# Sigmoid attention and a gated feed-forward on one core: four f chunks of the first batch done as seven block products, and a bank order in the late pairs

## The chip, the cores and the metric

One core of a Trainium2 chip runs the whole program; the other cores do nothing. The metric is the device time of one execution in microseconds (us). A core has a matrix engine (TensorE, PE in the profile; its weight loads are a row of their own, PEld), a vector engine (VectorE, DVE), a scalar engine (ScalarE, ACT), GpSimd (POOL), which here only issues DMAs and a tiny copy, and SyncE (SP), which issues the stores and the DMA transposes. Each engine works through its own instructions in the order in which the program gives them; semaphores tie the engines together. Matrix products land in PSUM, which this kernel uses as eight banks of 128 rows by 512 fp32 columns.

## The reference

```python
def _attn_ref(q, k, v):                      # 8 batches, 12 heads, 448 tokens, 64 deep
    S = q.shape[2]
    scale = 1.0 / np.sqrt(q.shape[-1])
    scores = scale * np.matmul(q, k.transpose(0, 1, 3, 2)) - np.log(S)
    attn = 1.0 / (1.0 + np.exp(-scores))
    return np.matmul(attn, v).astype(np.float32)

def _moe_ref(x, w_gate, w_val, w_out):       # 3584 tokens, 768 wide, 1536 inner
    gate = np.maximum(x @ w_gate, 0.0)
    val = x @ w_val
    return (gate * val @ w_out).astype(np.float32)

def reference(**kwargs):
    ...
    attn_out = _attn_ref(**attn_kwargs)
    B, H, S, D = attn_out.shape
    x = np.ascontiguousarray(attn_out.transpose(0, 2, 1, 3)).reshape(B * S, H * D)
    return _moe_ref(x=x, **moe_kwargs)
```

There is no softmax: each score goes through a sigmoid by itself. All inputs and the output are fp32; the kernel multiplies in fp16 and accumulates in fp32.

## The kernel before

**Attention.** A batch is 3 groups (g) of 4 heads by 7 chunks (c) of 64 keys for each half of the heads: 21 score units. `qk_unit` (L299) makes one: 4 matmuls of 64 by 64 by 448 columns (`qk`, L233) into two banks, and two sigmoids on ScalarE (L187) that write the tile PT. After a group's seven units `pv` (L249) multiplies PT with the values, 28 matmuls in 64-row pieces into two banks, and `put_xT` (L172) copies them to xT on VectorE (L184). Queries and keys are needed transposed: for batches 0 and 1 TensorE does that (`transposed`, L198; `both` is two calls of it), for later batches VectorE gathers them into a tile `rel` (L222, two buffers) and SyncE issues a DMA transpose of it (L226, `dma_transposes`).

**Feed-forward up.** The inner dimension is 12 chunks f of 128. For a chunk and a run of tokens the plain form is `gv` (L311): six matmuls for the gate product g_ps and six for the value product v_ps, one bank each (L322), a relu of g_ps into `gate_sb` on ScalarE (L334) or, when `act_relu` is false, on VectorE (L336), and one VectorE product of gate_sb and v_ps into hT (L343). Here this last one is called the gating product.

Most of it is done instead by a scheme that replaces eight block products by seven, with sums of blocks made beforehand on VectorE: for pairs of batches (`gv_pair`, L594), for the down projection (`down_pair`, L448), and for one batch alone, whose 448 tokens are cut into two halves of 224 (`gv_split`, L688). `gv_split` treats four f chunks at once. Gate and value weights are two block rows, the two halves of the 768 inputs are the block columns; the tokens' two halves are the columns of the other operand. It needs:

- `split_sums(b)` (L674): four sums of xT's blocks into a tile that takes one of xT's three buffers.
- weight sums, four steps for two chunks (`early_sum_steps`, L556): `gate_sums` replaces wv's upper half by wg − wv **in place**, then S2, S1 and S4. After the first of them a plain `gv` of these chunks is no longer possible. The sums take the SBUF of the first batch's old PT tiles.
- six banks, named u, g2 and g1 (p, c and a in the code), two each: every product is 12 matmuls of 224 columns, two chunks to a bank. The products are numbered by their weight set: 0, 3, 4, 1, 5, 6, 2. The products 0, 4, 5 and 2 add up in u, 3 and 6 in g2, 1 stands in g1. Between them the running values are copied out of the banks (`copy`, L719) or added to fp32 tiles `gsb` (`plus`, L723), and at the end four gating products (L729) write hT.

Before the change `gv_split` serves batch 1 alone: chunks 0 to 3 and 4 to 7, in batch 2's stretch. Batch 0 is done entirely in plain form.

**Banks.** `bank()` (L77) hands out the bank at the front of a ring of eight and moves it to the end; a new user waits for the last reader of the bank it gets. `later(order)` (L85) moves the named banks to the end again, so that they come back later. In the order list 0 to 7 are places in the ring, 7 the one handed out last.

**What stands beside what.** The main loop (L924) runs batch by batch. A batch's 21 score units are cut into bursts; behind each burst comes feed-forward work of earlier batches. For batch 1 (the *stretch* of this text) the cuts are after 3, 6, 9, 13, 17 and 21 units, with a `pv` inside the fourth and the sixth burst. Behind the bursts `ffn_mix` (L764) takes `mix` = 4, 3, 3, 3, 3, 4 plain units of batch 0 from a queue: four units of the second token half (192 tokens; the first half has 256) for f 0 to 3, then f 4 to 11 in pairs of chunks, first half and second half in turn. Two of them, (first half, f 9) and (second half, f 8), have their relu on VectorE. Between units `hooks` place the transposes of batch 1's groups (`both`) and batch 2's DMA transposes; `late_loads` (L863) does batch 2's third DMA transpose, a small copy on POOL that waits for the second (`hold`), and then issues batch 2's values, batch 3's keys and queries and w_out. `steps` and `given` spread the sixteen weight-sum steps, which batch 1's split work needs later, over the mixes in the order of the chunks.

**Loads.** All big loads are DMAs issued from POOL's queue in program order (L113, L115, L117, L149); `load_gv(f0, f1)` brings the gate and value weights of some chunks.

**Late pairs.** In batches 5 and 7 a `down_pair` is interrupted by a burst of three score units (`amid`). For the pairs in `SUMS_LATE` (L403) its tail is: product b with S3, an addition and a scaling of it on VectorE, a new bank d, `later((0, 7))`, the last two sum steps of the next pair, product d and its addition (L489 to L501). The next burst follows: two score units, a `pv`, two score units.

Of the kernel before, what the change touches and what calls it, by code (L numbers as in the profile page):

```python
# [18 lines left out]
def kernel(  # L19
# [10 lines left out]
    nc = tc.nc  # L30
# [46 lines left out]
    def bank(name, shape=(P, 512), dtype=FP32):  # L77
        pool, tag = free[0]
        free.rotate(-1)
        return pool.tile(list(shape), dtype, tag=tag, name=name)  # L80
# [4 lines left out]
    def later(order):  # L85
        keys = [free[i - 8] for i in order]
        for key in keys:
            free.remove(key)
            free.append(key)
# [55 lines left out]
    def load_gv(f0, f1, which=(0, 1)):  # L145
        fs = slice(f0 * P, f1 * P)
        for i in which:
            wt, src = ((wg, moe_w_gate), (wv, moe_w_val))[i]
            nc.gpsimd.dma_start(wt[:, :, fs], src[:, fs].rearrange("(c p) f -> p c f", p=P))  # L149
# [4 lines left out]
    load(1, 0, 1, "kq")  # L154
    load_gv(4, 6)
    load(1, 1, 2, "kq")
    load_gv(6, 9)
    load_v(1)
    load(1, 2, 3, "kq")
    load_gv(9, 12)  # L160

    def load_o():
        for f0, f1 in ((0, HF), (HF, NFC)):
# [186 lines left out]
    def store(g, t, ysb, m0, m1, engines):  # L350
        if len(engines) == 1:
            b, c = 2 * g + 2 * t // NCH, 2 * t % NCH
            dst = out[b * S : (b + 1) * S, m0:m1].rearrange("(t c) m -> c t m", c=NCH)[c : c + 2]
            engines[0].dma_start(dst, ysb[:, m0:m1])
            return
        for i, eng in enumerate(engines):
            j = 2 * t + i
            b, c = 2 * g + j // NCH, j % NCH
            dst = out[b * S : (b + 1) * S, m0:m1].rearrange("(t c) m -> c t m", c=NCH)[c]
            eng.dma_start(dst, ysb[64 * i : 64 * i + 64, m0:m1])  # L360
# [87 lines left out]
    def down_pair(g, p, beside, then, last, first_copy, amid=None):  # L448
# [14 lines left out]
        def plus(o, ps):  # L463
            nc.vector.scalar_tensor_tensor(  # L464
                out=o, in0=ps[:, 0:HM], scalar=OUT_SCALE, in1=o, op0=AOP.mult, op1=AOP.add
            )
# [6 lines left out]
        if (g, p) in SUMS_LATE:  # L473
            product(a, A12, B21)
            plus(y1[:, lo], a)
            product(c, S1, T1)
            scaled_act(y2[:, hi], c)
            product(b, S2, T2, False)
            scaled_act(y1[:, hi], b)
            product(c, S4, B22, False)  # L480
            plus(y1[:, hi], c)
            store(*first, y1, 0, DM, (nc.sync, nc.sync))
            steps = ()
            if amid:
                amid()
                steps = prepare_steps()
                for step in steps[:2]:
                    step()
            product(b, S3, T3, False)  # L489
            plus(y2[:, hi], b)  # L490
            (scaled if amid else scaled_act)(y2[:, lo], b)
            d = bank("y21")
            if amid:
                later((0, 7))
                for step in steps[2:]:
                    step()
            else:
                then()
            product(d, A22, T4)
            plus(y2[:, lo], d)  # L500
            store(*second, y2, 0, DM, (nc.sync, nc.sync))  # L501
            return
        product(c, S1, T1)
# [181 lines left out]
        sub(T4, B21, T2)  # L685
        sub(T3, B22, B12)

    def gv_split(b, f, beside):  # L688
        x = xT_tiles[b]
        T1, T2, T4, T3 = split_X[b]  # L690
        B11, B21, B22 = x[:, 0:HD, 0:SQ], x[:, HD:NDC, 0:SQ], x[:, HD:NDC, SQ:S]
        p, c, a = ([bank(nm) for _ in range(2)] for nm in ("u", "g2", "g1"))
        later((6, 7, 4, 5, 2, 3))
        gs = [[gsbp.tile([P, S], FP32, tag="gsb", name="gsb") for _ in range(3)] for _ in range(2)]
        h = hT_tiles[b // 2]
        sets = []
# [20 lines left out]
        def copy(i, ps, by=nc.scalar.copy):  # L717
            for u in range(2):
                by(gs[u][i][:], ps[u][:, 0:S])  # L719
# [12 lines left out]
            )  # L732

        product(p, 0, B11)
        copy(0, p, nc.vector.tensor_copy)
        product(c, 3, T1)
        copy(2, c)
        product(p, 4, T2, False)
        copy(1, p)
        beside()  # L740
        product(a, 1, B21)
        plus(0, a)
        product(p, 5, T3, False)
        plus(2, p)
        product(c, 6, B22, False)
# [14 lines left out]
    def push_first(half, fs, act_relu=True):  # L760
        c0, c1 = HALVES[half]
        push_gv(0, 64 * c0, 64 * (c1 - c0), fs, act_relu)
# [76 lines left out]
                after[(i, u)]()  # L839
    slots[5].pv()  # L840
    push_first(1, range(0, 4))
    for f0 in range(4, 12, 2):
        for half in range(2):
            for f in range(f0, f0 + 2):
                push_first(half, (f,), (half, f) not in ((0, 9), (1, 8)))


    order = [(g, c) for g in range(NG) for c in range(NCH)]
# [75 lines left out]
    for b in range(1, B):  # L924
# [10 lines left out]
        count = len(bursts)  # L935
        hooks = {}
        if b == 1:
            mix = (4, 3, 3, 3, 3, 4)
            hooks = {
                1: [(3, lambda: both(1, 1))],  # L940
                3: [(3, lambda: both(1, 2))],
                4: [(2, lambda: dma_transposes(2, 0)), (0, lambda: dma_transposes(2, 1))],
                5: [(4, late_loads)],
            }
            steps = itertools.chain.from_iterable(early_sum_steps(j, 2 * j) for j in range(4))
            given = ((0, 0, 1, 1, 1), (0, 1, 1, 1), (0, 1, 1, 1), (0, 1, 1, 0), (2, 0, 0, 0), (0, 1, 1, 1, 0))
        else:
            mix = (0,) * count

# [106 lines left out]
```

## Time and profile before

| | us |
|---|---|
| median of 3 executions | 389.37 (389.04 to 389.99) |
| the profiled execution | 388.7 |
| its span, first to last instruction | 386.9 |
| batch 1's stretch, first score product to batch 2's | 28.9 to 61.2 |

Busy time in parts of the span, from the view of windows (us):

| window | PE | DVE | ACT | POOL |
|---|---|---|---|---|
| 7.0 to 28.9 | 21.40 | 11.39 | 18.07 | 12.41 |
| 28.9 to 61.2 | 32.30 | 21.70 | 24.43 | 8.62 |
| 61.2 to 98.0 | 36.80 | 28.27 | 26.00 | 8.62 |
| 98.0 to 224.0 | 125.99 | 106.87 | 83.08 | 13.95 |

The granted TensorE clock is 1.00 in all of them. A matmul's recorded duration holds its way through the array, and matmuls overlap; what one costs is the distance from its start to the next one's start. The same holds for ScalarE and VectorE: the sigmoids of a burst overlap a little. In a timeline row stand the start, the length of the merged group, engine, line, operation, tiles and shapes, the count, and in brackets idle time before it and what ended it.

### The profile page before, as it was taken

To read this page: it belongs to the slowest core of one execution; us is meant where nothing else is said; L and a number is where in the kernel's file an instruction comes from. 1 tells how busy PE (TensorE), PEld (TensorE's weight loads), DVE (VectorE), ACT (ScalarE), POOL (GpSimd) and SP (SyncE) were. 2 spreads that over 40 slices of the span, in tenths; PEclk is the share of its full clock that TensorE was granted. 3 is DMA by queue.
4 is the path that set the end of the run, shared out by engine and by line. 5 is a ranking of instruction groups with operands and counts; after the bars stand their busy time and mean duration, and the time that the engine had idled before them with its cause. 6 is when DMAs were issued, how large, how long until landed. Compare 5 with 4: busy or idle time off the path is not lost.

```text
span 386.9 us, 8977 instructions
## 1 busy us (share of the span) xinstructions
PE 381.3 (99%) x3570; PEld 224.8 (58%) x3570; DVE 304.3 (79%) x609; ACT 227.5 (59%) x480; POOL 49.9 (13%) x73
## 2 busy tenths in 40 slices
PE   8999999999999999999999999999999999999995
PEld 6688776885555545555555554545555555555563
DVE  3455667769868999999867789999987788999563
ACT  5967887567777645555777764545577344333321
POOL 9543306100400003000300300000000000000000
PEclk9999999999999999999999999999999999999999
DMA  9999999999969303972599893222012220000336
GB/s 177 197 199 204 203 192 162 208 208 128 184 148 193 81 2 38 156 120 47 50 230 223 160 232 56 49 48 50 0 43 71 69 69 0 2 0 0 83 88 160
DMA packets 67421, 43.81 MB, mean 113 GB/s; under 512 B 35634, under 2 KB 64050, under 8 KB 67378
## 3 DMA queue, kind: packets, MB, share of 16 engines
q0 software_dynamic: 28960, 23.24, 39.9%
q1 hardware_dynamic: 37634, 19.24, 24.7%
q10 hardware_dynamic: 784, 0.75, 0.6%
q8 instruction: 28, 0.46, 0.5%
q14 instruction: 15, 0.12, 0.1%
HBM read 47.19 MB, written 11.01 MB: 150 GB/s over the span
## 4 chain that ended last, share of the span: by engine, by line
PE 97%; ACT 2%; DVE 0%; issue 0%
PE u L385 35%; PE g L385 16%; PE y L385 12%; PE qk_ps L239 10%; PE pv_ps L257 8%; PE g_ps L322 5%; PE v_ps L322 5%; PE u L708 2%; PE g L708 2%; ACT PT L187 2%; PE warm_ps L175 1%; PE trt L204 1%; DVE ysb L540 0%; DVE zeros L130 0%
## 5 line engine op out<-in xcount | busy, mean ns | idle before, releaser
L187 ACT ACTIVATE PT<-qk_ps 128x448 f16<-128x448 f32 (+3 forms) x318 | 151.2, 583 | 78.8 <-PE qk_ps L239 78.6
L385 PEld LDWEIGHTS <-S 128*128 128x128 f16 x576 | 56.4, 98 | 45.9
L624 DVE TENSOR_TENSOR gsb<-g,gsb 128x448 f32<-128x448 f32 x72 | 42.8, 624 | 8.0 <-PE g L385 7.7
L239 PE MATMUL qk_ps<-qkT 64*64 64x448 f16 (+2 forms) x756 | 47.8, 336 | 0.5 <-ACT PT L187 0.3
L385 PEld LDWEIGHTS <-hT 128*128 128x128 f16 x318 | 29.5, 98 | 24.0 <-issue 6.1
L257 PE MATMUL pv_ps<-PT,v 64*64 64x448 f16 (+2 forms) x756 | 37.0, 329 | 0.0
L464 DVE SCALAR_TENSOR_TENSOR ysb<-y,ysb 128x384 f32<-128x384 f32 x33 | 18.3, 555 | 20.8 <-PE y L385 14.3
L184 DVE TENSOR_SCALAR xT<-pv_ps 128x448 f16<-128x448 f32 (+2 forms) x53 | 27.8, 567 | 8.2 <-PE pv_ps L257 7.1
L385 PEld LDWEIGHTS <-wg 128*128 128x128 f16 x216 | 20.2, 98 | 21.8 <-issue 4.3
L385 PEld LDWEIGHTS <-wv 128*128 128x128 f16 x216 | 21.1, 98 | 19.7
L446 ACT ACTIVATE ysb<-u 128x384 f32<-128x384 f32 x28 | 13.8, 491 | 30.6 <-PE u L385 26.5
L239 PEld LDWEIGHTS <-qkT 64*64 64x64 f16 x756 | 18.3, 106 | 20.3 <-issue 13.8
L385 PE MATMUL u<-wo,hT 128*128 128x384 f16 x156 | 29.8, 327 | 0.0
L111 POOL DMA_DIRECT2D k<-in_k_dram x14 | 10.8, 775 | 141.6 <-DVE rel L222 136.0
L257 PEld LDWEIGHTS <-v 64*64 64x64 f16 x756 | 22.5, 107 | 10.3 <-issue 1.1
L385 PE MATMUL u<-xT,wg 128*128 128x448 f16 x108 | 23.5, 354 | 0.0
L385 PE MATMUL g<-X,S 128*128 128x448 f16 x108 | 23.4, 352 | 0.0
L385 PE MATMUL u<-xT,wv 128*128 128x448 f16 x108 | 23.4, 352 | 0.0
L385 PE MATMUL u<-X,S 128*128 128x448 f16 x108 | 23.4, 352 | 0.0
L385 PE MATMUL g<-xT,wg 128*128 128x448 f16 x108 | 23.4, 353 | 0.0
L385 PE MATMUL u<-X,wv 128*128 128x448 f16 x108 | 23.4, 352 | 0.0
L385 PE MATMUL g<-xT,S 128*128 128x448 f16 x108 | 23.4, 352 | 0.0
(98 smaller groups left out, 563.5 us busy)
## 6 DMA issues: line engine op xcount, KB each, us to landing
out_dram<-ysb SPq DMA_DIRECT2D x50, 192.0 KB, 3.9
v<-in_v_dram POOLq DMA_DIRECT2D x8, 336.0 KB, 15.7
v<-in_v_dram POOLq DMA_DIRECT2D x16, 168.0 KB, 15.4
k<-in_k_dram POOLq DMA_DIRECT2D x4, 672.0 KB, 12.3
q<-in_q_dram POOLq DMA_DIRECT2D x4, 672.0 KB, 15.6
wo<-in_moe_w_out_dram POOLq DMA_DIRECT2D x2, 1152.0 KB, 19.0
k<-in_k_dram POOLq DMA_DIRECT2D x9, 224.0 KB, 11.9
q<-in_q_dram POOLq DMA_DIRECT2D x7, 224.0 KB, 12.3
```

Source lines behind the costliest of these rows:

```text
L111: nc.gpsimd.dma_start(t16[:, xs, cs], rows_of(src, b)[:, xs, cs])
L175: nc.tensor.matmul(ps[:, 0:n], zeros[:, 0:P], zeros[:, 0:n], start=True, stop=True)
L184: nc.vector.tensor_scalar(out=xT, in0=src, scalar1=XSCALE, scalar2=None, op0=AOP.mult)
L187: nc.scalar.activation(PT_ap, ps_ap, AF.Sigmoid, bias=sig_bias, scale=qk_scale)
L239: nc.tensor.matmul(out_of(hh)[o : o + 64, :], qkT[rows, c, cols], qkT[rows, NCH + c0 : NCH + c1, cols], start=True, stop=True, tile_positi ...
L257: nc.tensor.matmul(ps[hh][64 * r : 64 * r + 64, 0:qn], v16[rows, 2 * g + hh, c * D : (c + 1) * D], pieces[c][rows, hh, :], start=(c == 0), ...
L322: nc.tensor.matmul(ps[:, 0:qn], (wg, wv)[i][:, dc, f * P : (f + 1) * P], xT_tiles[b][:, dc, q0 : q0 + qn], start=(dc == 0), stop=(dc == ND ...
L385: nc.tensor.matmul(ps[:, 0:n], A[:, k_, :], W[:, k_, :], start=(first and k_ == 0), stop=(k_ == kn - 1), skip_group_check=True,)
L446: nc.scalar.activation(o, ps[:, 0:HM], AF.Copy, scale=OUT_SCALE)
L464: nc.vector.scalar_tensor_tensor(out=o, in0=ps[:, 0:HM], scalar=OUT_SCALE, in1=o, op0=AOP.mult, op1=AOP.add)
L624: nc.vector.tensor_tensor(out=gs[u][i][:], in0=ps[u][:, 0:S], in1=gs[u][i][:], op=AOP.add)
L708: nc.tensor.matmul(ps[j // 2][:, j % 2 * SQ : (j % 2 + 1) * SQ], sets[j][i][:, k_, :], W[:, k_, :], start=(first and j % 2 == 0 and k_ == ...
```

## The change

It does in batch 1's stretch four chunks of batch 0, f 4 to 7 with all 448 tokens, by `gv_split` (behind the third burst), in place of eight plain units. The mixes become 2, 1, 1, 2, 3 and 3 units; the queue holds f 0 to 3 of the second half, then f 8 and 9 and f 10 and 11 for both halves, all with the relu on ScalarE. `split_sums(0)` goes ahead of the first unit. The sum steps come in the order of chunks 4, 6, 0, 2, since chunks 4 to 7 are used first and chunks 0 to 3 must stay plain until their units are done; the last four steps for f 6 stand around the start of the split work. For this use `gv_split` gets a variant, `sums_late`: products in the order 0, 1, 3, 4, 5, 6, 2, the copy of product 0 on ScalarE, and the banks asked for and put back in another order. The hooks move: `both(1, 2)` stays behind the fourth burst, the first two DMA transposes of batch 2 stand after two and three of the fifth mix's three units (before: after one and three), `late_loads` stays at the head of the sixth mix. Weights are loaded as chunks 6 to 7, 8 to 9 and 10 to 11 in place of 6 to 8 and 9 to 11.

In the late pairs `later((0, 7))` becomes `later((0, 6, 7))`, and the next pair's last two sum steps come behind the addition of product d instead of ahead of product d.

```diff
-    load_gv(6, 9)
+    load_gv(6, 8)
     load_v(1)
     load(1, 2, 3, "kq")
-    load_gv(9, 12)
+    load_gv(8, 10)
+    load_gv(10, 12)
...
             d = bank("y21")
             if amid:
-                later((0, 7))
-                for step in steps[2:]:
-                    step()
+                later((0, 6, 7))
             else:
                 then()
             product(d, A22, T4)
             plus(y2[:, lo], d)
+            for step in steps[2:]:
+                step()
             store(*second, y2, 0, DM, (nc.sync, nc.sync))
             return
...
-    def gv_split(b, f, beside):
+    def gv_split(b, f, beside, sums_late=False):
...
-        p, c, a = ([bank(nm) for _ in range(2)] for nm in ("u", "g2", "g1"))
-        later((6, 7, 4, 5, 2, 3))
+        if sums_late:
+            p, a, c = ([bank(nm) for _ in range(2)] for nm in ("u", "g1", "g2"))
+            later((4, 5, 6, 7, 2, 3))
+        else:
+            p, c, a = ([bank(nm) for _ in range(2)] for nm in ("u", "g2", "g1"))
+            later((6, 7, 4, 5, 2, 3))
...
         product(p, 0, B11)
-        copy(0, p, nc.vector.tensor_copy)
+        copy(0, p, nc.scalar.copy if sums_late else nc.vector.tensor_copy)
+        if sums_late:
+            product(a, 1, B21)
+            plus(0, a)
+            beside()
         product(c, 3, T1)
         copy(2, c)
         product(p, 4, T2, False)
         copy(1, p)
-        beside()
-        product(a, 1, B21)
-        plus(0, a)
+        if not sums_late:
+            beside()
+            product(a, 1, B21)
+            plus(0, a)
         product(p, 5, T3, False)
...
-    for f0 in range(4, 12, 2):
+    for f0 in (8, 10):
         for half in range(2):
-            for f in range(f0, f0 + 2):
-                push_first(half, (f,), (half, f) not in ((0, 9), (1, 8)))
+            push_first(half, (f0, f0 + 1))
...
         if b == 1:
-            mix = (4, 3, 3, 3, 3, 4)
+            mix = (2, 1, 1, 2, 3, 3)
+            steps = itertools.chain.from_iterable(early_sum_steps(j, 2 * j) for j in (2, 3, 0, 1))
+
+            def some_sums(n):
+                for step in itertools.islice(steps, n):
+                    step()
+
+            def first_split():
+                some_sums(3)
+                gv_split(0, 4, lambda: some_sums(1), True)
+
             hooks = {
-                1: [(3, lambda: both(1, 1))],
-                3: [(3, lambda: both(1, 2))],
-                4: [(2, lambda: dma_transposes(2, 0)), (0, lambda: dma_transposes(2, 1))],
-                5: [(4, late_loads)],
+                0: [(2, lambda: split_sums(0))],
+                1: [(1, lambda: both(1, 1))],
+                2: [(0, first_split)],
+                3: [(2, lambda: both(1, 2))],
+                4: [(1, lambda: dma_transposes(2, 0)), (0, lambda: dma_transposes(2, 1))],
+                5: [(3, late_loads)],
             }
-            steps = itertools.chain.from_iterable(early_sum_steps(j, 2 * j) for j in range(4))
-            given = ((0, 0, 1, 1, 1), (0, 1, 1, 1), (0, 1, 1, 1), (0, 1, 1, 0), (2, 0, 0, 0), (0, 1, 1, 1, 0))
+            given = ((0, 0, 1), (1, 1), (1, 0), (0, 1, 1), (1, 1, 0, 1), (0, 1, 1, 1))
```

## The prediction

> **What bounds the kernel now.** I read the page's busy times and chain of waits first, then the timelines of TensorE (PE), ScalarE (ACT) and VectorE (DVE) through batch 1's stretch, 28.9 to 61.2 us, and TensorE's around the pairs that the second edit touches.
>
> ```profile
> PE 381.3 (99%) x3570; PEld 224.8 (58%) x3570; DVE 304.3 (79%) x609; ACT 227.5 (59%) x480; POOL 49.9 (13%) x73
> ...
> PE 97%; ACT 2%; DVE 0%; issue 0%
> ```
>
> The chain is TensorE almost alone, so a product left out is worth its time and a wait put in front of TensorE costs its time. The change does both. First TensorE: two plain products of 256 and of 192 columns, the existing split work of batch 1, and two weighted-sum rounds (pv) followed by eight score products (qk).
>
> ```profile
> 36.59 0.82 PE L322 MATMUL g_ps<-xT,wg 128*128 128x256 f16 x6
> 37.24 0.82 PE L322 MATMUL v_ps<-xT,wv 128*128 128x256 f16 x6
> 37.90 0.66 PE L322 MATMUL g_ps<-xT,wg 128*128 128x192 f16 x6
> 38.39 0.66 PE L322 MATMUL v_ps<-xT,wv 128*128 128x192 f16 x6
> ...
> 66.48 1.32 PE L708 MATMUL u<-xT,wg 128*128 128x224 f16 x12
> 67.64 1.31 PE L708 MATMUL g<-X,S 128*128 128x224 f16 x12
> 68.79 1.31 PE L708 MATMUL u<-X,S 128*128 128x224 f16 x12
> ...
> 182.91 1.49 PE L257 MATMUL pv_ps<-PT,v 64*64 64x448 f16 x28
> 184.24 0.55 PE L239 MATMUL qk_ps<-qkT 64*64 64x448 f16 x8
> 184.72 1.15 PE L385 MATMUL u<-wo,hT 128*128 128x384 f16 x6
> ...
> 192.85 1.62 PE L257 MATMUL pv_ps<-PT,v 64*64 64x448 f16 x28
> 194.17 0.68 PE L239 MATMUL qk_ps<-qkT 64*64 64x448 f16 x8
> 194.78 1.15 PE L385 MATMUL u<-wo,hT 128*128 128x384 f16 x6
> ```
>
> Start to start counts, since a group's length holds its drain: 0.655 us for a 256-column product, 0.495 for 192, 1.15 for twelve 224-column matmuls. Then the two engines that empty the banks:
>
> ```profile
> 29.39 2.72 ACT L187 ACTIVATE PT<-qk_ps 128x448 f16<-128x448 f32 x6 [0.62 <-PE qk_ps L239]
> 31.96 0.83 ACT L334 ACTIVATE gate_sb<-g_ps 128x192 f32<-128x192 f32 x3
> ...
> 50.32 3.60 ACT L187 ACTIVATE PT<-qk_ps 128x448 f16<-128x448 f32 x8 [0.59 <-PE qk_ps L239]
> ```
>
> ```profile
> 32.38 0.62 DVE L343 TENSOR_TENSOR hT<-gate_sb,v_ps 128x192 f16<-128x192 f32 x2 [2.62 <-ACT gate_sb L334]
> ...
> 51.77 0.42 DVE L336 TENSOR_SCALAR gate_sb<-g_ps 128x256 f32<-128x256 f32 x1 [0.34 <-PE g_ps L322]
> ...
> 52.76 0.39 DVE L222 COPY rel<-k 128x896 f16<-128x896 f16 x1
> ...
> 58.18 0.40 DVE L222 COPY rel<-k 128x896 f16<-128x896 f16 x1 [0.80 <-DMA qkT<-rel]
> ```
>
> Sigmoids follow each other by (31.96 − 29.39)/6 = 0.43 us, and a relu of a unit waits its turn behind all sigmoids of the burst before it. VectorE's gating product waits for that relu (2.62 us here) and everything behind it on VectorE waits too. Today four-unit mixes give TensorE enough to do meanwhile, and in the burst of eight sigmoids VectorE takes the relus itself (51.77).
>
> **Term 1, products removed.** Eight units, 4 × 2 × (0.655 + 0.495) = 9.20 us, become seven products, 7 × 1.15 = 8.05: **−1.15 us**. Bursts, and with them the 0.1 us at each turn between 64- and 128-row work, stay six.
>
> **Term 2, ring order.** From 192.85 to the u product is 1.93 us, from 182.91 it is 1.81: the pv's second bank is that of the burst's sixth sigmoid, which ends at 192.91. The same 0.12 to 0.13 stands at 202.91 and 289.93. The new order gives pv the bank that VectorE's scaling empties at 192.60; the step sums, 0.47 each, then run behind the last addition, before pv's own copies at 194.38. 3 × 0.13 = **−0.39 us**; bounds 0 and −0.4.
>
> **Term 3, waits added.** The trace shows none of the new stretch, so I walk it bank by bank: eight banks handed round, each engine in program order, with spacings 0.43 us a sigmoid, 0.21 and 0.26 a relu, 0.19 a score unit, 0.27 and 0.33 a gating product. The same walk over today's order ends at 61.05 where the trace has 61.11 (the 61.20 start less the 0.1 turn).
>
> (a) *Second burst.* Until 31.6 nothing differs. Two units now stand between the bursts instead of four, so the second burst starts at 31.69. Its second score unit needs the banks of sigmoids five and six, ended 32.12 and known at TensorE 0.05 later (wanted 31.88); its third needs the first unit's, freed by the gating product of 32.38 + 0.35 = 32.73, known at 32.79 (wanted 32.36). 0.29 + 0.43 = **+0.72**, nearly read off the trace.
>
> (b) *S1 of chunks 6 and 7.* ScalarE goes from sigmoids to sigmoids: the third burst's six begin at 35.5, its relu comes at 38.0, the gating product ends at 38.7. Only then may VectorE do the three steps that open the split work (gate sums, S2, S1). Each reads the one before, and then an operation starts 0.03 us after its predecessor's end (X's sums start at 64.21 and 64.74, 0.50 long), so 0.55 + 0.03 each: S1 is there at 40.4. TensorE starts the split at 36.7, and 2 × 1.15 + 0.58 later, 39.5, wants it: **+0.88**.
>
> (c) *Products 4 and 5.* Both add into u and stand next to each other now; batch 1's version has the g1 product between. Half of product 4 is done 0.17 (drain) + 0.07 after its issue, ScalarE's copy takes 0.58 (L719's mean) + 0.06 to tell: 0.88, of which product 4's other half covers 0.58: **+0.30**. Bounds 0 and 1.15.
>
> (d) *Sixth burst.* All relus are ScalarE's now. The fifth burst's eight sigmoids, from 52.2, end their turn at 55.6; VectorE stands before the first gating product until 56.0, then has a sum step, then the second product, done 57.1. The sixth burst's pv wants that bank at 56.6: **+0.54**.
>
> (e) *Into batch 2.* Behind that same product stand the copies for batch 2's first DMA transpose: 57.0 to 57.7 instead of 52.8 to 53.4. The third pair of copies needs the first's buffer, free when that transpose has landed, some 4.6 us later (53.45 to 58.18 today, idle 0.80): VectorE stands from 60.2 to 62.3. Queued behind are the gating products of units (0,11), (1,10), (1,11), so batch 2's first burst waits for their banks: 0.90 at its second score unit, 0.54 at its pv, **+1.44**. With the shortest landing (3.97, the row of 58.95 to 62.92) it is 0.96; with 5 us it is 1.9, batch 2's first scores then waiting for the transpose as well.
>
> Other edits cost nothing. split_sums of batch 0 (four of 0.53) fit in VectorE's 2.62 us of idling before 32.38; else +0.5 in (a). Weight chunks 6 and 7 land before today's 37.34 since a smaller transfer comes first, and are read at 38.7; chunks 8 to 11, with one more issue pair on POOL's queue (0.84 each), are used from 49 on, and today land at 49.09 as a set ending in 12. The hold, batch 2's values, batch 3's keys and queries and w_out on POOL move by up to 3 us; w_out then lands near 89.5 and is first read after 92.1. ScalarE's six extra copies and VectorE's additions are in the walk.
>
> Sum: 0.72 + 0.88 + 0.30 + 0.54 + 1.44 = +3.88; −1.15 − 0.39 leaves **+2.3 us**. The span would be 386.9 + 2.3 = 389.2; that execution took 388.7, 1.8 more than its span, and the median is 389.37, so I forecast **391.7 us**.
>
> **Rivals.**
> *No change.* VectorE is late, but TensorE doesn't feel it: (d) and (e) are there only if the sixth burst's pv and batch 2's first burst draw the banks that gating products empty. One place further round they would draw banks that ScalarE's relu or sigmoid emptied long before, and 1.98 of the sum is gone: +2.3 − 2.0 = +0.3, 389.7, not slower as measured. For it: the split work hands the ring back in a new order, which no row shows. Against: counted through, that order is two spare banks, then g1's, g2's and u's, and the count from there is even. From one bank's shift on it decides. 0.17.
> *It does what it says.* The shorter mixes are covered, sums and copies come in time: −1.54, 387.8. For it: ScalarE is busy 24.4 of the stretch's 32.3 us, VectorE 21.7, so neither is full. Against: (a), which needs one trace row. 0.11.
> *The clock falls.* TensorE idles briefly at bank after bank. The 22 warm-up matmuls of 194 columns take 3.74 us, 0.17 each, where 192 columns later take 0.08: if one such slow stretch returned, half of it, 1.9 us, would be added: 393.6. Against: the granted clock is 1.00 through 7 to 28.9 us, where TensorE waited 0.33 us at 9.8. 0.04. The Trainium skill ("TensorE: Matmul & The Clock Gate", A second HAM failure mode: psum-queue depth-cycling) says that micro-idling between groups while banks cycle makes the clock fall and rise; by that rule this rival happens, and the trace so far does not agree.
> *The forecast* stands from the point where the first transpose's copies end after 55.6 (60.2 less 4.6; today 53.45, in the walk 57.7): 0.68; its own range is 390.7 to 392.6.
>
> **Chances and range.** About 0.3%, 1.2 us, is what measuring this kernel can tell from no change. Slower: 0.68 less a twentieth for its lower end, and the clock's 0.04: 0.69. Same: 0.17 and that remainder: 0.20. Faster 0.11. The range runs from the no-change rival with a little room, 389.4, to 392.9, (e)'s and (c)'s upper bounds; outside lie the faster case, the clock and the tails.
>
> **What would show it.** The L708 group in 28 to 50 us with 84 matmuls and a gap of about 0.9 in its third product; a VectorE wait for the DMA transpose of 2 us near 60 instead of 0.80; batch 2's first u product near 69 instead of 66.5; pv rounds at three late pairs 1.81 us to the next u. If TensorE runs the stretch without gaps and batch 2 starts before 61, the walk is wrong.

## The result, and the profile after

The changed kernel takes **391.88 us** (median of 6 executions, 391.29 to 393.37) against 389.03 (388.71 to 389.99) for the kernel before on the same chip: ratio 1.0084, 95% interval 1.0072 to 1.0096. It is slower by 2.85 us. Its profiled execution took 391.74 us with a span of 389.2, 2.3 more than the span before.

Lines of the changed kernel stand one to five further down: L239 is now L240, L257 is L258, L343 is L344, L708 is L713, L719 is L724. From its page, the busy times and the chain of waits:

```profile
PE 381.4 (98%) x3558; PEld 222.7 (57%) x3558; DVE 308.6 (79%) x613; ACT 228.3 (59%) x480; POOL 51.4 (13%) x75
...
PE 90%; DMA 5%; ACT 2%; DVE 1%; POOL 1%; issue 0%; POOLq 0%; DVEq 0%; ACTq 0%
```

TensorE is as busy as before (381.3) with twelve matmuls fewer, and 98% instead of 99% of a longer span. The chain, 97% TensorE before, now leaves it for a tenth: where TensorE stood, the view follows whoever released it. That tenth is no measure of the stops: 15.9 us of it are two loads ahead of 19.2 us, where TensorE stood 0.41 us, and 5.5 us are one DMA transpose issued at 209.6. Where TensorE stood is in its timeline through batch 1's stretch (start, length, engine, line, operation, tiles, shapes, count; idle time in brackets); the last three rows are the first late pair, where the stop is gone:

```profile
31.61 1.47 PE L240 MATMUL qk_ps<-qkT 64*64 64x448 f16 x12
33.01 0.58 PE L205 MATMUL trt<-ident,k 128*64 128x128 f16 x14
...
36.71 1.31 PE L713 MATMUL u<-xT,wg 128*128 128x224 f16 x12
37.86 1.31 PE L713 MATMUL g<-xT,wg 128*128 128x224 f16 x12
39.01 0.74 PE L713 MATMUL g<-X,S 128*128 128x224 f16 x6
40.49 0.75 PE L713 MATMUL g<-X,S 128*128 128x224 f16 x6 [0.74 <-DVE S L574]
41.07 1.31 PE L713 MATMUL u<-X,S 128*128 128x224 f16 x12
42.43 1.31 PE L713 MATMUL u<-X,wv 128*128 128x224 f16 x12
43.58 1.31 PE L713 MATMUL g<-xT,S 128*128 128x224 f16 x12
...
56.20 0.67 PE L240 MATMUL qk_ps<-qkT 64*64 64x448 f16 x8
56.61 0.42 PE L258 MATMUL pv_ps<-PT,v 64*64 64x448 f16 x2
57.22 1.51 PE L258 MATMUL pv_ps<-PT,v 64*64 64x448 f16 x26 [0.20 <-DVE hT L344]
...
62.44 0.56 PE L240 MATMUL qk_ps<-qkT 64*64 64x448 f16 x5
63.33 0.38 PE L240 MATMUL qk_ps<-qkT 64*64 64x448 f16 x3 [0.33 <-DVE hT L344]
63.34 0.53 PE L258 MATMUL pv_ps<-PT,v 64*64 64x448 f16 x2
64.06 1.51 PE L258 MATMUL pv_ps<-PT,v 64*64 64x448 f16 x26 [0.20 <-DVE hT L344]
...
68.95 1.32 PE L713 MATMUL u<-xT,wg 128*128 128x224 f16 x12
...
195.47 1.49 PE L258 MATMUL pv_ps<-PT,v 64*64 64x448 f16 x28
196.79 0.55 PE L240 MATMUL qk_ps<-qkT 64*64 64x448 f16 x8
197.27 1.15 PE L386 MATMUL u<-wo,hT 128*128 128x384 f16 x6
```

The brackets understate the stops, because a matmul's recorded length holds its drain; starts tell the cost. The second burst's twelve score matmuls take 33.01 − 31.61 = 1.40 us, where the undisturbed third burst's take 0.70. The third product's halves lie 1.48 apart instead of 0.58. Product 4 takes 42.43 − 41.07 = 1.36 instead of 1.15. Batch 1's own split work starts at 68.95; before, it did at 66.48. What TensorE waited for there stands in the timelines of ScalarE and VectorE:

```profile
35.44 2.73 ACT L188 ACTIVATE PT<-qk_ps 128x448 f16<-128x448 f32 x6
38.00 0.39 ACT L335 ACTIVATE gate_sb<-g_ps 128x192 f32<-128x192 f32 x1
```

```profile
38.42 0.35 DVE L344 TENSOR_TENSOR hT<-gate_sb,v_ps 128x192 f16<-128x192 f32 x1 [1.77 <-ACT gate_sb L335]
38.69 0.55 DVE L377 TENSOR_TENSOR wv<-wg,wv 128x768 f16<-128x768 f16 x1
39.28 0.56 DVE L377 TENSOR_TENSOR S<-wv 128x768 f16<-128x768 f16 x1
39.87 0.56 DVE L574 TENSOR_TENSOR S<-S,wg 128x768 f16<-128x768 f16 x1
...
56.08 0.35 DVE L344 TENSOR_TENSOR hT<-gate_sb,v_ps 128x192 f16<-128x192 f32 x1 [2.62 <-ACT gate_sb L335]
...
62.25 0.39 DVE L223 COPY rel<-k 128x896 f16<-128x896 f16 x1 [2.00 <-DMA qkT<-rel]
```

VectorE stands 1.77 us for a relu that ScalarE gets to only at 38.00, behind a burst of six sigmoids, then does gate sums, S2 and S1 one after the other, ending at 39.87 + 0.56 = 40.43; TensorE's half product starts at 40.49. It stands 2.62 us before the fifth burst's first gating product, and 2.00 for the first DMA transpose of batch 2 (0.80 before).

### The profile page after: what moved, and what is told of

It is laid out like the page before. It is cut to its first block, busy times and chain, and to the rows that moved or that the text cites. A ratio compares the mean times of both kernels' runs of the same rounds, so it can differ in the third digit from the quotient of the medians.

```text
span 389.2 us, 8951 instructions
## 1 busy us (share of the span) xinstructions
PE 381.4 (98%) x3558; PEld 222.7 (57%) x3558; DVE 308.6 (79%) x613; ACT 228.3 (59%) x480; POOL 51.4 (13%) x75
## 4 chain that ended last, share of the span: by engine, by line
PE 90%; DMA 5%; ACT 2%; DVE 1%; POOL 1%; issue 0%; POOLq 0%; DVEq 0%; ACTq 0%
PE u L386 34%; PE g L386 16%; PE y L386 12%; PE qk_ps L240 8%; PE pv_ps L258 8%; PE g_ps L323 3%; PE u L713 3%; PE v_ps L323 3%; DMA wv<-in_moe_w_val_dram 3%; PE g L713 2%; DMA k<-in_k_dram 1%; DMA qkT<-rel 1%; ACT PT L188 1%; PE trt L205 1%; DVE S L377 0%
## 5 line engine op out<-in xcount | busy, mean ns | idle before, releaser
L240 PE MATMUL qk_ps<-qkT 64*64 64x448 f16 (+2 forms) x756 | 48.7, 336 | 1.1 <-DVE hT L344 0.3
L258 PE MATMUL pv_ps<-PT,v 64*64 64x448 f16 (+2 forms) x756 | 37.6, 329 | 0.4 <-DVE hT L344 0.4
L240 PEld LDWEIGHTS <-qkT 64*64 64x64 f16 x756 | 18.5, 105 | 22.2 <-issue 15.2
L258 PEld LDWEIGHTS <-v 64*64 64x64 f16 x756 | 21.7, 107 | 11.8 <-issue 1.9
```

The costliest lines, as they stand in the source:

```text
L240: nc.tensor.matmul(out_of(hh)[o : o + 64, :], qkT[rows, c, cols], qkT[rows, NCH + c0 : NCH + c1, cols], start=True, stop=True, tile_positi ...
L258: nc.tensor.matmul(ps[hh][64 * r : 64 * r + 64, 0:qn], v16[rows, 2 * g + hh, c * D : (c + 1) * D], pieces[c][rows, hh, :], start=(c == 0), ...
```

## The experiments

Every median is given beside that of the kernel before in the same comparison (x_t0, x_sums, x_relu and x_ring share one with 388.65, x_all and x_v one with 388.86, x_hold, x_allhold and x_bhold one with 388.81). For batch 1's stretch the measure is the **distance** from the start of the new split work to the start of batch 1's split in the last stretch, 68.95 − 36.71, before rounding 32.25 us, in the changed kernel; it leaves out what differs ahead of 28.9 us from one execution to the next. The five waits between those two points ((b) to (e), as numbered in the prediction) are taken away one at a time, then all together.

**x_t0: an earlier first transpose, against (e).**

```diff
-                4: [(1, lambda: dma_transposes(2, 0)), (0, lambda: dma_transposes(2, 1))],
+                4: [(3, lambda: dma_transposes(2, 0)), (0, lambda: dma_transposes(2, 1))],
```

> The changed kernel with one hook moved: the copies for batch 2's first DMA transpose stand ahead of the fifth mix's first unit (at 3 left) instead of behind its second (at 1 left). Theory (waits in order): VectorE makes them at about 52.9 while it would stand before the gating product at 56.1 anyway; the third pair of copies then finds its buffer free, the idling of 2.00 us before it goes, and the two waits of batch 2's first burst (0.49 and 0.36 idle in the trace, 1.2 to 1.4 of start) go with it: batch 1's split work starts at 67.5 instead of 68.95, the time falls by 1.4 to 390.4. The sixth burst's wait at 57.2 stays. Rival (VectorE and ScalarE are simply too full): the wait moves elsewhere and the split starts at 68.6 or later.

Distance 31.01, **1.24 less**; both waits of batch 2's first burst are gone and the one at 57 stays. Time 391.19 beside 388.65, ratio 1.0061 (1.0049 to 1.0073). The profiled execution also stood 1.84 us at 122.65, where the changed kernel's had stood 0.14; that is taken up below.

**x_sums: three sum steps ahead of the last plain unit before the split, against (b).**

```diff
             def first_split():
-                some_sums(3)
                 gv_split(0, 4, lambda: some_sums(1), True)
...
-            given = ((0, 0, 1), (1, 1), (1, 0), (0, 1, 1), (1, 1, 0, 1), (0, 1, 1, 1))
+            given = ((0, 0, 1), (1, 1), (4, 0), (0, 1, 1), (1, 1, 0, 1), (0, 1, 1, 1))
```

> The changed kernel with the gate sums, S2 and S1 of chunks 6 and 7 placed ahead of the last plain unit before the split instead of behind it, so that VectorE makes them in the 1.77 us in which it waits for that unit's relu. Theory (waits in order): the 0.74 us idle of TensorE (0.88 of start) in product 3 goes, nothing else changes: batch 1's split starts at 68.1 instead of 68.95, the time falls by 0.9 to 391.0. Rival (too full): the gating product of that unit comes later, holds a bank, and less than a third is gained: 68.65 or later.

Distance 31.34, **0.90 less**, and the stop inside the third product is gone. Time 391.49, ratio 1.0072 (1.0048 to 1.0096).

**x_relu: one relu back on VectorE, against (d).**

```diff
-            push_first(half, (f0, f0 + 1))
+            for f in (f0, f0 + 1):
+                push_first(half, (f,), (half, f) not in ((1, 8), ))
```

> The changed kernel with the relu of the fifth mix's first unit (second half, chunk 8) on VectorE, as before the change, instead of on ScalarE behind the eight sigmoids. Theory (waits in order): VectorE no longer stands until 56.1, the sixth burst's pv finds its bank (its 0.54 goes), the copies for the first transpose come at about 56.5 instead of 57.1, and batch 2's first burst loses 0.2 of its 1.4: the split starts at 68.2, the time falls by 0.7 to 391.1. Rival (too full): 68.65 or later.

Distance 31.51, **0.74 less**. The pv of the sixth burst runs undisturbed, and 0.10 us of (e) goes with it. Time 390.67, ratio 1.0066 (1.0043 to 1.0090).

The distances of these three runs came out about as expected, the largest miss being the 0.2 of x_t0. The times did not: 391.19, 391.49 and 390.67 stand where 390.4, 391.0 and 391.1 were expected. The profiled executions of all three stood 1.5 to 2.2 us near 122, which is more than each edit gains, so a single edit is read from the distance and not from the time.

**x_order: product 4 ahead of product 3, against (c) and most of (b).**

```diff
+        if sums_late:
+            product(p, 4, T2, False)
+            copy(1, p)
         product(c, 3, T1)
         copy(2, c)
-        product(p, 4, T2, False)
-        copy(1, p)
         if not sums_late:
+            product(p, 4, T2, False)
+            copy(1, p)
```

> After with product 4 of the new split ahead of product 3, nothing else. Theory (products 4 and 5 next to each other in one bank wait for the copy between them, 0.30 us at 42.43, and product 3's sums, which come late, get 1.5 us more, which hides most of the 1.00 us wait at 40.49): batch 1's split of the last stretch starts 31.2 to 31.6 us after the new split instead of 32.25, and the two waits together fall from 1.30 to at most 0.5 us. Rival (VectorE is full there and everything it does slides by as much): the distance falls by less than 0.3 us.

Distance 31.49, **0.76 less**. Of the stops of (b) and (c) one is left, inside product 4, 40.33 − 38.85 − 1.15 = 0.33 us:

```profile
38.85 1.63 PE L713 MATMUL u<-X,S 128*128 128x224 f16 x12
40.33 1.31 PE L713 MATMUL g<-X,S 128*128 128x224 f16 x12
```

One execution gave 390.42 us.

**x_loads: the weight loads as before.**

```diff
-    load_gv(6, 8)
+    load_gv(6, 9)
...
-    load_gv(8, 10)
-    load_gv(10, 12)
+    load_gv(9, 12)
```

> After with the weight loads split as in the kernel before (chunks 6 to 8 ahead of batch 1's values, 9 to 11 behind the third group, instead of 6 and 7, then 8 and 9, 10 and 11). Theory (the gate sums of chunks 6 and 7 start late because VectorE comes to them late, not because their weights land late): the distance between the two splits stays 32.2 us within 0.15, the wait at 40.49 included. Rival (the wait at 40.49 hangs on the landing of the weights): that wait grows by 0.5 us or more, since the larger load lands later.

Distance 32.28, the stop at 40.73 is 0.90: the loads have no part in it. One execution gave 391.60 us.

**x_all: the waits of the stretch all at once.** x_t0's edit with the second transpose at unit 2, x_sums, x_relu, x_order, and for (a) the first unit of the second half with its relu on VectorE:

```diff
-    push_first(1, range(0, 4))
+    push_first(1, (0,), False)
+    push_first(1, range(1, 4))
...
-                4: [(1, lambda: dma_transposes(2, 0)), (0, lambda: dma_transposes(2, 1))],
+                4: [(3, lambda: dma_transposes(2, 0)), (2, lambda: dma_transposes(2, 1))],
```

> After with every wait that the trace of after has in batch 1 taken away where it starts: gate, S2 and S1 sums of chunks 6 and 7 ahead of the third product's plain unit; product 4 ahead of product 3 in the new split, so that products 4 and 5 no longer follow each other in one bank; the relus of the second half's chunk 8 and of its chunk 0 on VectorE; the two DMA transposes of batch 2 hooked at units 3 and 2 of the fifth product instead of 1 and 0. Theory (five waits made the loss, each about as large as the prediction's terms, and the seven products do save 1.15 us): batch 1's split of the last stretch starts at 65.5 to 66.0 us in the profile, 0.5 to 1.0 before the kernel before (66.48) and 3.0 to 3.4 before after (68.95), with no TensorE wait over 0.1 us between 33.5 and 66; the time 387.7 to 389.0, faster than after by 2.9 to 4.1 us and than before by 0 to 1.3, as far as the variable waits near 120 and 214 us (0 to 2.2 us together in the profiles so far) let it. Rival (ScalarE and VectorE are too full for the extra sums and copies in that stretch, so a wait taken away at one place comes back at another): the split starts at 67.5 us or later and the time stays over 390.

Distance 29.25, **3.00 less**, against (b) to (e) of 0.90 + 0.21 + 0.64 + 1.23 = 2.98 in the changed kernel's rows. TensorE's timeline, where 40.49, 57.22, 63.33 and 64.06 stood with brackets above:

```profile
36.65 1.31 PE L713 MATMUL u<-xT,wg 128*128 128x224 f16 x12
37.80 1.31 PE L713 MATMUL g<-xT,wg 128*128 128x224 f16 x12
38.95 1.31 PE L713 MATMUL u<-X,S 128*128 128x224 f16 x12
40.10 1.31 PE L713 MATMUL g<-X,S 128*128 128x224 f16 x12
...
55.43 1.49 PE L258 MATMUL pv_ps<-PT,v 64*64 64x448 f16 x28
...
60.63 0.57 PE L240 MATMUL qk_ps<-qkT 64*64 64x448 f16 x8
61.03 1.49 PE L258 MATMUL pv_ps<-PT,v 64*64 64x448 f16 x28
...
65.90 1.32 PE L713 MATMUL u<-xT,wg 128*128 128x224 f16 x12
```

Ahead of the new split, (a)'s burst takes 1.08 us instead of 1.40, so that 0.39 of its 0.71 is still there. Batch 1's split starts at 65.90, 0.58 ahead of the kernel before; counted from the start of the stretch, 65.90 − 29.05 = 36.85 beside 66.48 − 28.91 = 37.57, it is 0.72. The engines are not too full: the waits (b) to (e) came from the order of the work and from which engine did a relu. Time 388.60 beside 388.86, ratio 0.9997 (0.9980 to 1.0013): not told apart from before, although 0.72 here and 0.39 at the late pairs should show. In the profiled execution 0.34 us was lost at 119.5 and 0.60 at 212.7.

**x_ring: the late pairs' part alone, on the kernel before.**

```diff
             if amid:
-                later((0, 7))
-                for step in steps[2:]:
-                    step()
+                later((0, 6, 7))
...
             plus(y2[:, lo], d)
+            for step in steps[2:]:
+                step()
```

> The kernel before with the late pairs' part of the change alone: the bank order and the place of the last two sum steps. Theory: the waits of the pv at 192.85, 202.91 and 289.93 go, 0.13 each, nothing else moves: from those pv to the next u product 1.81 us instead of 1.93, the span is 386.5 instead of 386.9, and the time 388.6 where the kernel before has 389.0. Rival (the part does nothing, or its sum steps come late to the next pair): the span stays at 386.9 or grows, with a new wait in the next pair's product with S1.

The three stops are gone: pv to the next u product is 1.80 and 1.81. Yet the time is 388.60 beside 388.65, ratio 1.0004 (0.9995 to 1.0013). The profiled execution lost 0.79 us at 120.35 and 0.85 at 213.76, though this kernel is the one before up to 190 us, whose profile has no stop at the first place and 0.09 at the second.

**x_v: what stops TensorE near 122.** In the changed kernel's profile VectorE stands before the scaled copy into `ysb` (L442) until the store of the first late pair of batches 0 and 1 has landed. The try was to load batch 4's values later:

```diff
-                jobs.append(lambda: load_v(b + 1))
+                if b != 3:
+                    jobs.append(lambda: load_v(b + 1))
...
-                jobs.append(lambda: dma_transposes(4, 1))
+                jobs.append(lambda: (dma_transposes(4, 1), load_v(4)))
```

> After with one edit: the loads of batch 4's values are issued in batch 3's last stretch (near 121 us) instead of its first (101 to 103 us). Theory (the stores issued from 108 us on stand behind these loads in the DMA engines: in five profiles the second store landed 4.8 to 6.8 us after the last value load, at 118.7 to 124.9 us, and the third late pair's first scaled copy waits for it, 0.14 to 2.2 us of TensorE): the stores issued near 108 to 109 us land before 116, the TensorE wait near 122 us is 0 in the profile, and the time falls by 0.3 to 1.0 us against after, to 390.8 to 391.5 on this chip; batch 1's split of the last stretch stays at 68.9 to 69.0 us, since nothing before 98 us changes. Rival (the stores are late because of the transposes of batch 3 and the key and query loads, or of the memory itself): the stores still land after 119 us, the wait stays and the time is that of after.

It misses. POOL issues the load at 101.03 us as before: nothing stands ahead of it in POOL's queue, so a later place in the text alone delays nothing. So the run is a second profile of the changed kernel's order of work: 392.85 us beside 388.86, ratio 1.0085 (1.0051 to 1.0118), distance 32.23, with the stop near 122 at 2.3 us where the changed kernel's profile had 0.14. VectorE's line, then TensorE's:

```profile
123.62 0.56 DVE L442 TENSOR_SCALAR ysb<-u 128x384 f32<-128x384 f32 x1 [2.36 <-DMA out_dram<-ysb]
```

```profile
120.98 1.14 PE L386 MATMUL y<-T,S 128*128 128x384 f16 x6
124.24 2.06 PE L386 MATMUL u<-T,S 128*128 128x384 f16 x6 [2.12 <-DVE ysb L442]
126.09 1.93 PE L386 MATMUL y<-wo,S 128*128 128x384 f16 x6
127.96 0.76 PE L240 MATMUL qk_ps<-qkT 64*64 64x448 f16 x12
```

These rows show a second cost: the two products behind the stop take 2.06 and 1.93 us where the one ahead of it takes 1.14. The view of windows gives the granted TensorE clock in its third column from the right:

```profile
124.29:127.70 3.41, 3.41 (x12) 1.51 (x11) 2.73 (x7) 0.98 (x2) 0.00 (x0) 0.50 0.62 136
```

The clock is at one half for 3.41 us, from just behind the stop, and at 1.00 again after it. From the u product to the next score product it is 127.96 − 124.24 = 3.72 us; in the changed kernel's profile the same work takes 124.41 − 122.37 = 2.04. So this execution, the slowest of its five with 394.92 us, lost 1.68 us to the clock besides the stop itself. No other profile of this case shows it inside the work: in x_relu a stop of 2.2 us at the same place left the clock at 1.00. What decides it is not shown.

**x_hold, x_allhold, x_bhold: the same, with something to wait for.**

```diff
-                jobs.append(lambda: load_v(b + 1))
+                if b not in (3, 5):
+                    jobs.append(lambda: load_v(b + 1))
...
-                jobs.append(lambda: dma_transposes(4, 1))
+                jobs.append(lambda: (dma_transposes(4, 1), hold(4, 0), load_v(4)))
...
-                jobs += [lambda: dma_transposes(6, 0), lambda: dma_transposes(6, 1)]
+                jobs += [lambda: dma_transposes(6, 0), lambda: dma_transposes(6, 1), lambda: (hold(6, 0), load_v(6))]
```

On the changed kernel:

> After with the value loads of batches 4 and 6 held on POOL until the first DMA transpose of the same batch has landed (a copy of two of its elements ahead of the load, as the kernel does for batch 2); the last try only moved the load in the text, and POOL, which had nothing ahead of it, issued it at 101 us as before. Theory (the stores issued from 108 us on stand behind the value loads, which land at 114 to 121 us; the store of the first late pair lands 4.8 to 6.8 us behind them and the third pair's scaled copy waits for it): the value loads of batch 4 are issued after 123 us, the stores issued near 108 to 109 us land before 117, the TensorE wait near 122 us (0.14 in after's profile, 1.5 to 2.3 in four others of its family) is gone, the wait near 215 us for the transposes of batch 6 is at most 0.2, and the time is 390.8 to 391.4 us, 0.4 to 1.0 under after's; batch 1's split stays 32.2 us behind the new split. Rival (the stores are late because of the key and query loads and the transposes of batch 3): the first stores land after 119 us all the same, the wait stays somewhere in its 0.1 to 2.3 us, and the time stays at 391.5 to 392.5.

390.98 us beside 388.81, ratio 1.0060 (1.0048 to 1.0073), distance 32.27. The loads go out at 125.9 and 214.2 us, and no stop over 0.1 us is left behind 64 us. The time came out as expected, one step did not: the first stores land at 119.0, not before 117, which is the landing that the rival had named; but the wait is gone all the same. The view of DMA from 104 to 128 us, in forty slices of 0.6 us (tenths of 16 engines busy, and GB/s), the changed kernel first:

```profile
DMA  9999999999999999961111113999987963999990
GB/s 85 98 199 211 203 206 200 206 211 197 209 199 208 215 292 321 284 142 40 40 45 53 51 51 97 225 328 251 230 261 199 139 80 53 278 286 239 291 228 0
```

```profile
DMA  9999999999968865111111114998887999999816
GB/s 89 75 186 205 214 196 211 199 208 193 135 123 174 184 143 130 77 51 51 51 51 51 56 51 123 220 328 225 169 258 169 155 188 241 223 223 217 170 4 45
```

In both there is a stretch in which one to two tenths of sixteen engines, two or three of them, are busy at 40 to 56 GB/s while the rest stand: a transfer on few engines. With the values out of the way it starts sooner (slice 16 against 18), but it is still there. By its issue at 107.7 and its size it should be the one store of 384 KB (L355), the one that VectorE waits for; the trace has no landing for it. In x_hold only stores are in flight there: at 51 GB/s its 384 KB take some 7.7 us, an estimate from its size and that row, and the stores of 108.6 and 109.2 land behind it, at 119.0 and 119.5. The Trainium skill ("DMA: Bandwidth & Descriptors", Why a DMA increments its semaphore by 16 and not by 1) says that a DMA uses the largest number of engines up to 16 that divides the outermost dimension of both sides; this store's target has an outermost dimension of 2, and the row of two or three busy engines agrees. That storing it otherwise would help was not tried.

With x_all's edits, all of batch 1's waits away but for 0.39 us of (a):

> The kernel with all of batch 1's waits taken away (seven products kept, split of the last stretch at 65.90 us, 388.6 us) with the same two holds. Theory: split of the last stretch at 65.5 to 66.0 us, no TensorE wait over 0.1 us between 90 and 230 us, time 387.3 to 388.1 us, faster than before by 0.6 to 1.6 us (0.57 of the split, 0.39 of the late pairs and what the variable waits gave back). Rival (the variable waits have another source): they stay, 0.3 to 2 us together, and the time stays at 388.4 to 388.9, the same as before.

**387.66 us** beside 388.81, ratio 0.9979 (0.9969 to 0.9989), 1.15 us faster than the kernel before, and 4.2 under the changed kernel's 391.88, which is from another comparison. Distance 29.25 again, no stop over 0.1 us behind 33.2 us; the split starts at 66.22, since this execution came to its stretch 0.3 later. On the kernel before, with the late pairs' part:

> The kernel before with the late pairs' part of the change and the same two holds. Theory: the three waits of 0.13 us at the late pairs and the variable waits near 120 and 214 us are all gone, the split of the last stretch stays at 66.3 to 66.5 us, and the time is 388.0 to 388.4 us, 0.3 to 0.7 below before. Rival (the variable waits have another source): the time is that of the run with the late pairs' part alone, within 0.2 of before.

388.24 us, ratio 0.9984 (0.9975 to 0.9993), no stop near 120 or 214. x_hold differs from it by the change in batch 1's stretch and its weight loads alone: 390.98 − 388.24 = 2.74 us, beside 2.54 in the rows of the changed kernel.

From x_allhold it differs by the seven products with (b) to (e) gone. In the traces these are worth 0.70 us: from the start of the stretch to batch 1's split it is 66.22 − 29.36 = 36.86 there and 66.22 − 28.66 = 37.56 here. The medians differ by 388.24 − 387.66 = 0.58 us, but their intervals overlap. The two profiled executions have the same span, 386.3, since x_allhold's came to its stretch 0.70 later. So that the seven products gain anything over the eight units is shown in the traces, not in time.

**x_holdonly: the holds without the late pairs' part.**

> The kernel before with the two holds alone, without the late pairs' part, to part the two gains of the last run of that family (388.24 us, ratio 0.9984 with both). Theory (the late pairs' order is worth its three waits of 0.13 us, 0.39 together, once nothing near 120 and 214 us gives them back): the three waits of 0.13 us are in the profile again, near 193, 203 and 290 us, no wait near 120 or 214 us is over 0.1 us, and the time is 388.4 to 388.8 us, ratio 0.999 to 1.000. Rival (the holds make the whole gain, and the late pairs' order is worth nothing in time): the time is 388.2 to 388.3, ratio 0.998 to 0.9985.

388.68 beside 389.16, ratio 0.9991 (0.9981 to 1.0001). Nothing stops near 120 or 214, and the late pairs stop as before (from pv to u it is 194.57 − 192.63 = 1.94):

```profile
192.63 1.62 PE L257 MATMUL pv_ps<-PT,v 64*64 64x448 f16 x28
193.96 0.68 PE L239 MATMUL qk_ps<-qkT 64*64 64x448 f16 x8
194.57 1.15 PE L385 MATMUL u<-wo,hT 128*128 128x384 f16 x6
```

The ratios differ by 0.0007, 0.27 us, which fits 0.39, but the intervals overlap: in time the order of the late pairs is not shown to be worth anything, in the traces it is.

## Why the prediction was right, step by step

The forecast was 391.7 us, a span of 389.2 and batch 1's split near 69; they came out at 391.88, 389.2 and 68.95. That the time itself is only 0.2 us off is in part luck: the forecast adds 2.3 to a median of 389.37, the kernel before took 389.03 in this comparison, 0.34 less, and the step was 2.85, 0.55 more. What was right is the mechanism, term by term, from starts in the two profiles:

| step | predicted | measured | how |
|---|---|---|---|
| Term 1, products | −1.15 | −1.15 | 36.71 to the next burst at 45.97 is 9.26, less stops of 0.90 and 0.21, less the 0.1 turn: 8.05, where eight units were 9.20; in x_all, without stops, 44.79 − 36.65 − 0.1 = 8.04 |
| Term 2, ring order | −0.39 | −0.39 in the trace, not shown in time | pv to u 197.27 − 195.47 = 1.80, was 1.93, three times |
| (a) second burst | +0.72 | +0.71 | 1.40, was 0.69 |
| (b) S1 late | +0.88 | +0.90 | 1.48 less 0.58; x_sums −0.90 |
| (c) products 4 and 5 | +0.30 | +0.21 | 1.36 less 1.15 |
| (d) sixth burst | +0.54 | +0.64 | 56.20 to 59.05, the next product, is 2.85, was 2.21 |
| (e) into batch 2 | +1.44 | +1.23 | 62.44 to 65.88, likewise, is 3.44, was 2.21; x_t0 −1.24 |

The waits add up to +3.69 where the walk said +3.88; (c), (d) and (e) were off by 0.09, 0.10 and 0.21, and part of that cancels. (e) is the term that was mis-sized most: VectorE was let go at 62.25 where the walk had 62.3, which is 0.05 of it. At the second score unit 0.63 was waited instead of 0.90 (62.65 to 63.33 between two matmuls that else start 0.05 apart), at the pv 0.60 instead of 0.54; why was not traced further. The term stays over the 0.96 that the prediction gave as its lower end. One thing that was to cost nothing moved further than thought: batch 2's value loads went from 60.45 to 65.43, 5.0 us and not up to 3; no stop shows behind that between 69 and 122 us.

(b), (d) and (e) each have a run of their own: taking away the cause took away that wait and, but for 0.10 of (e) that went with (d), nothing else of the stretch. (c) was taken away only together with most of (b), and (a) only in x_all and in part. Taking (b) to (e) away together gave 3.00 for 2.98. That rules out, for these four, the rival tested with them, that ScalarE and VectorE are simply too full. The rival of no change hung on which banks the two bursts draw; the brackets on `hT L344` at 57.22, 63.33 and 64.06 show that they draw the gating products' banks, as counted. The rival that the clock falls did not happen in the changed kernel's profile: the granted clock is 1.00 over the span, with stops of up to 0.9 us between and inside groups. The Trainium skill's rule on banks being cycled ("TensorE: Matmul & The Clock Gate", A second HAM failure mode: psum-queue depth-cycling) would have had it fall and rise; this trace does not agree. The clock did fall once in this family, in x_v, behind a stop of 2.3 us near 122, and it cost 1.68 us there, where the prediction priced such a stretch at 1.9; the prediction looked for it among the short stops at the banks.

The sum of the measured terms is 3.69 − 1.15 = 2.54 up to the split at 68.95, and the stretch began 0.08 sooner (28.83 for 28.91): 2.46. The span agrees for one more reason that was not in the sum. The changed kernel is 2.47 late at 68.95, gains 0.39 at the late pairs, and loses 0.14 at 122.37 and, against the 0.09 of the kernel before, 0.14 more at 215.16: 2.36, beside 2.3 of span. The two last stops, for a store and for a DMA transpose, the prediction did not have; that they are small in the profiled execution is luck. In four other profiles without the holds (x_t0, x_sums, x_relu and x_v) the first is 1.5 to 2.3 us, in x_loads and x_order 0 and 0.24. So the median, +2.85 where +2.3 was forecast, probably holds some of them: the spans of its six executions run from 389.2 to 391.5, the profiled one being the shortest, and the holds, which take them away, bring 391.88 to 390.98, ratio 1.0084 to 1.0060, though from two comparisons whose intervals just touch. The forecast leaves 391.7 − 389.2 = 2.5 us between span and time, since it adds to the median and not to the profiled execution, where that was 1.8; in the changed kernel's profiled execution it was 2.5. Over all the profiled runs it is 1.7 to 2.8, in no order that follows the kernels, so that this agreement is chance.

What makes the stop near 122 long in one execution and short in another is narrowed down, not settled: in x_v the DMA transpose issued near 98 us and the last of the value loads behind it landed 1.7 and 4.2 us later than in the changed kernel's profile, from the same instructions.

## What to carry to other kernels

A faster formula in a stretch where two other engines empty the banks is worth its matmuls only if the order of relus, sums, copies and transposes is laid out again with it: here 1.15 us saved stood against 3.69 of waits, of which all but 0.4 went away by reordering and by giving two relus to VectorE, with no work removed. Walk the ring bank by bank, each engine in program order, before believing such a change; starts, not bracketed idle times, give what a stop costs. A long stop can cost more than its length, so read the clock behind it. And moving a load later in the text does nothing on a queue that has nothing else to wait for; it needs a wait of its own.

## What the runs showed of the hardware that was not expected

- The same instructions differ from run to run in how their DMAs land: the stop near 122 us was 0.14 us in one profile of the changed kernel's sequence and 2.3 in another. A change of 0.4 us at the late pairs was not told apart in time, neither beside these stops nor with the holds.
- One store of 384 KB moved at 40 to 56 GB/s with two or three DMA engines busy, where the loads before it moved at about 200. In the changed kernel it was issued at 107.84 us and let VectorE go at 121.75, 13.9 later, part of it behind the loads. The two stores of 192 KB issued right behind it took 13.4 and 13.3 us, where the median of the page's row for that size is 2.9.
- With the values out of their way the transposes of batch 6 landed 4.2 and 4.5 us after their issue instead of 5.5 and 5.3.
- Behind a stop of 2.3 us TensorE's granted clock was 0.50 for 3.41 us in one execution (x_v), which made 2.04 us of work 3.72. Stops of 0.9 us (the changed kernel) and of 2.2 us (x_relu) left it at 1.00.
